# Turning every x chunk by DMA transpose, with the k weights on one queue, and moving the last LayerNorm tile and the w4 load

## The chip, the cores and the metric

The kernel runs on one core of a Trainium2 chip. The metric is the device time of one execution in microseconds (us), as measured for each run. The profiled execution also has a "span", the time from its first to its last recorded work; it is 1.5 to 2 us shorter than the measured time of the same run. All runs told of here were correct, and all are fast runs, that is, no run was over 1.5% above the fastest of the same kernel.

## The reference

The function mixes a linear attention branch A and a feed-forward branch B of the same input x by a sigmoid gate. S is 2048, D is 640, H is 32 heads of 20, F is 1728; everything is bf16.

```python
x = A_x                                       # [1, 2048, 640]
g = sigmoid((x * gate_w).sum(-1, keepdims=True))

# branch A
q, k, v = heads(x @ wqkv)                     # wqkv [640, 1920]
pq, pk = phi(q), phi(k)                       # phi(t) = where(t > 0, t + 1, exp(t)) + 1e-6
kv  = einsum("bhsd,bhse->bhde", pk, v)
z   = einsum("bhsd->bhd", pk)
num = einsum("bhqd,bhde->bhqe", pq, kv)
den = einsum("bhqd,bhd->bhq", pq, z)[..., None] + 1e-6
a   = merge_heads(num / den) @ wo

# branch B (its x is also A_x)
h  = gelu(layernorm(x) @ w1)
hs = shift_four_column_groups(h) @ w2         # rows shifted by +1, -1, +2, -2
x1 = x + hs
b  = x1 + gelu(layernorm(x1) @ w3) @ w4

return g * a + (1 - g) * b
```

## The kernel before

x is cut into 16 chunks of 128 rows, and into 4 tiles of 4 chunks. The k stage is `k = x @ wk`, and it needs x turned (`xT`, the 640 columns on the partitions) and wk in 5 pieces of 128 rows (`wk 0` to `wk 4`). It also produces the gate's logits, as a 641st column of wk that is filled from the gate vector `g5`. Below are the parts that matter; `sp`, `aq`, `gq` are the DMA queues of SP, ACT and POOL, and `pair()` gives one of 4 PSUM pairs (PSUM is the memory that matmuls write to). In the views PE runs the matmuls, DVE and ACT the elementwise work. LN1 is the LayerNorm of x and LN2 that of x1; their outputs `ln` are turned by DMA into `lnxT`. `den` is the denominator of the attention, `r_bf` its reciprocal, and an m unit computes one fifth of the product of `kv` and `wo`. The flight of a load is its time from issue to landing.

```python
    def load_x(c0, c1):        # plain load of chunks c0..c1, rows on partitions
        sp.dma_start(x_sb[:, c0:c1, 0:D], x2[c0 * P:c1 * P, :].rearrange("(c p) d -> p c d", p=P))
    def load_xT(c0, c1):       # DMA transpose of chunks c0..c1
        sp.dma_start_transpose(xT[:, :, c0 * P:c1 * P], x2[c0 * P:c1 * P, :])
    def load_wk(q, dc):        # one piece of wk, 160 KB
        q.dma_start(wk_sb[:, dc, 0:D], A_wqkv[dc * P:(dc + 1) * P, D:2 * D])

    load_x(0, 1)
    aq.dma_start(g5[:], gate_w.rearrange("(c p) -> c p", p=P))
    load_wk(sp, 1)
    load_wk(aq, 0)
    load_wk(aq, 2)
    load_wk(sp, 3)
    load_wk(aq, 4)
    for c0, c1 in ((1, 2), (2, 3), (3, 4), (4, 6), (6, 8), (8, 12), (12, 16)):
        load_xT(c0, c1)
    # ... wq, the rest of x, wv, w1, wo, w2, w3, all on sp

    def k_mm(pt, c, dcs, hfs=(0, 1), last=DC - 1):
        for dc in dcs:
            for hf in hfs:
                n = HD + hf
                nc.tensor.matmul(pt[:, hf, 0:n], lhsT=xT[:, dc, c * P:(c + 1) * P],
                                 rhs=wk_sb[:, dc, hf * HD:hf * HD + n], start=(dc == 0), stop=(dc == last))
    # ...
    warmup(6)                  # matmuls of ones, so that PE is busy while the loads fly
    warmup(3, P)
    kp = pair()
    # ... five PE transposes of x chunk 0 with two DVE copies into xT, and the gate vector turned by PE
    warmup(3, P)
    for dc in range(DC):
        k_mm(kp, 0, (dc,))
        if dc < DC - 1:
            warmup(1, 2 * P)
    k_evac(kp, 0)
    for c in range(1, NCH):
        pt = pair()
        k_mm(pt, c, range(DC))
        k_evac(pt, c)
    # ... the q stage, then the g stage (pk^T x), with LN1 of tiles 0 to 2 beside it

    def den_evac(pt):
        nc.scalar.activation(pt[:, 1, :], pt[:, 0, :], ACT.Copy, bias=1e-6)
        with nc.allow_low_precision(reason="rounded after a float32 division, as a copy would"):
            nc.vector.reciprocal(r_bf[:], pt[:, 1, :])

    def ln1_apply(c):          # "work" has 4 buffers
        # ...
        lnx = work.tile([P, D], BF16, name="ln")
        nc.vector.tensor_scalar(lnx[:], x_sb[:, c, 0:D], mv1[:, c, 0:1], rstd1[:, c:c + 1],
                                op0=ALU.subtract, op1=ALU.mult)
        nc.sync.dma_start_transpose(lnxT[t][:, :, cc * P:(cc + 1) * P], lnx[:])
    # ...
    for fcs in w1_split:
        w1_unit(0, fcs)
    kv_unit()
    den_evac(den_mm())
    for fcs in w1_split:
        w1_unit(1, fcs)
    for cc in range(CPT):
        ln1_apply(3 * CPT + cc)        # LN1 of the last tile
    s1.close()                 # frees the SBUF that w4_sb takes over
    # ... w4_sb allocated
    nc.gpsimd.dma_start(w4_sb[:, 0:FF, :], B_w4[0:FF * P, :].rearrange("(c p) f -> p c f", p=P))
    # ... two more loads for the rest of w4
    for j in range(DC):
        m_unit(j)              # each takes a PSUM pair; the second reuses den's
    r_unit()                   # reads r_bf
    # ... w2, w3, attention, w4 stages
```

## Time and profile before

| | before |
|---|---|
| time, median of 3 runs | 267.38 us (267.1 to 267.68) |
| span of the profiled run (266.56 us) | 264.9 us |
| PE busy | 260.5 us, 98% |
| first k matmul, chunk 0 done, chunk 1 done | 4.83, 7.19, 8.56 us |
| k stage ends, q stage begins on the chain | 27.80 us |
| reciprocal of den | 80.25 to 83.60 us |
| w2 stage begins | 88.28 us |

These lines are from the page of the kernel before: the busy time of the engines, the share by engine of the chain of waits (from the last instruction back, at each step to what released it), and the group of the k matmuls (busy us and mean ns of one, then the idle time just before them).

```profile
span 264.9 us, 4267 instructions
...
PE 260.5 (98%) x1744; PEld 162.6 (61%) x1744; DVE 139.6 (53%) x270; ACT 84.3 (32%) x122; POOL 22.7 (9%) x58
...
PE 97%; ACT 1%; DVE 0%; issue 0%
...
L190 PE MATMUL pp<-wk_sb,xT 128*128 128x320 bf16 (+1 forms) x160 | 23.0, 303 | 0.0
```

The kernel is a stream of matmuls. PE stood idle for 0.0 us before its 160 k matmuls. So no load was late for PE. What PE does at the start that is not useful are the warm-up matmuls.

The chain of waits of before, in order of time, shows the two places where the stream could be denser. Its columns are start us, us, and what.

```profile
0.83 3.04 PE pp L202 x9
...
5.03 0.54 PE pp L190 x2
...
7.09 20.71 PE pp L190 x152
27.80 21.58 PE pp L232 x100
...
85.03 0.69 PE pp L379 x16
85.74 2.49 ACT m_sb L381 x4
88.28 5.59 PE pp L415 x40
```

From 0.83 to 5 us (mostly cut here) there are only warm-ups and PE transposes. Then the five steps of chunk 0 run with a warm-up between each, and from 7.09 us on 152 k matmuls run without a break. At 85.7 us the chain is with ACT, which evacuates the m units.

The stretch from 3 to 5 us in the view by stretches shows what the DMA engines do while wk lands. The columns used here are the first (the stretch) and the last two: the mean busy share of the 16 DMA engines and what they moved in GB/s.

```profile
3.00:5.00 2.00, 2.00 (x15) 1.40 (x14) 0.71 (x3) 1.03 (x1) 1.67 (x6) 1.00 1.00 348
```

In this stretch the engines moved 348 GB/s.

The view of the tile wk_sb in before gives the flights of the five wk loads, shortest, median and longest:

```profile
DMA to landing us min/median/max: 3.1/3.8/4.0
```

The timeline of DVE around the reciprocal, before (start us, us, engine, line, operation, out<-in):

```profile
80.25 3.36 DVE L254 RECIPROCAL r_bf<-pp 128x512 bf16<-128x512 f32 x1
...
86.92 1.16 DVE L297 TENSOR_SCALAR ln<-x_sb,mv,rstd 128x640 bf16<-128x640 bf16 x3
88.28 0.45 DVE L297 TENSOR_SCALAR ln<-x_sb,mv,rstd 128x640 bf16<-128x640 bf16 x1 [0.20 <-DMA lnxT<-ln]
```

The reciprocal comes first and ends at 83.60. The four LN passes of the last tile come after it.

### The profile page before, as it was taken

Reading aid. Unit: us, or ns where it says so; the run is one execution under the profiler, and the core shown is the slowest. Engines: PE = TensorE matmul, PEld = TensorE weight load, DVE = VectorE, ACT = ScalarE, POOL = GpSimd, SP = SyncE. Lnnn points to the kernel's source line nnn. Section 1 sums busy time; section 2 is a strip of 40 time slices with the busy share of each in tenths; the row PEclk is TensorE's granted clock in tenths of the full one; section 3 lists DMA queues with packets and bytes.
Section 4 is the critical chain, followed back from the end, with each engine's and each line's share of the span. In section 5 each row is a group of like instructions: output and inputs, shape, how many; then the busy total and the mean of one; then the engine's idle time right before and its main releaser. Section 6 shows DMA issues by size and latency. Waiting matters only on the chain.

```text
span 264.9 us, 4267 instructions
## 1 busy us (share of the span) xinstructions
PE 260.5 (98%) x1744; PEld 162.6 (61%) x1744; DVE 139.6 (53%) x270; ACT 84.3 (32%) x122; POOL 22.7 (9%) x58
## 2 busy tenths in 40 slices
PE   8999999999999999999999999999999999999994
PEld 4777555788754644555666556567555566455663
DVE  1688778899856797955412364503464413122132
ACT  1555544321165635622420313330222340333100
POOL 7100010012223140001000001000001000000000
PEclk9999999999999999999999999999999999999999
DMA  7999989015668952000132000042000042000011
GB/s 194 148 182 350 369 293 330 9 33 121 125 97 217 228 105 52 0 0 2 25 74 77 25 0 2 11 88 77 25 0 2 1 99 74 27 0 2 0 50 50
DMA packets 44749, 23.62 MB, mean 89 GB/s; under 512 B 35450, under 2 KB 43642, under 8 KB 44730
## 3 DMA queue, kind: packets, MB, share of 16 engines
q1 hardware_dynamic: 43792, 20.57, 32.6%
q0 software_dynamic: 496, 2.29, 2.9%
q10 hardware_dynamic: 442, 0.49, 0.5%
q8 instruction: 13, 0.21, 0.3%
q14 instruction: 6, 0.05, 0.1%
HBM read 12.21 MB, written 2.62 MB: 56 GB/s over the span
## 4 chain that ended last, share of the span: by engine, by line
PE 97%; ACT 1%; DVE 0%; issue 0%
PE pp L479 22%; PE pp L462 21%; PE pp L190 8%; PE pp L307 8%; PE pp L415 8%; PE pp L446 8%; PE pp L341 8%; PE pp L232 8%; PE pp L202 2%; PE pp L467 1%; PE pp L488 1%; ACT m_sb L381 1%; PE pp L360 1%; PE pp L247 0%; PE pp L379 0%; PE pp L211 0%
## 5 line engine op out<-in xcount | busy, mean ns | idle before, releaser
L470 ACT ACTIVATE h<-pp 128x1024 bf16<-128x1024 f32 (+1 forms) x28 | 27.8, 993 | 102.8 <-PE pp L462 94.4
L462 PE MATMUL pp<-lnxT,w_sb 128*128 128x512 bf16 x260 | 60.4, 379 | 0.0
L479 PE MATMUL pp<-w_sb,h 128*128 128x320 bf16 x416 | 57.9, 299 | 0.0
L479 PEld LDWEIGHTS <-h 128*128 128x128 bf16 x416 | 40.0, 98 | 17.0 <-issue 1.9
L462 PEld LDWEIGHTS <-w_sb 128*128 128x128 bf16 x260 | 25.5, 98 | 26.7
L495 DVE SCALAR_TENSOR_TENSOR oc<-pp,omg,x 128x640 bf16<-128x640 f32 x15 | 12.9, 882 | 44.0 <-PE pp L488 27.1
L449 DVE SCALAR_TENSOR_TENSOR x<-pp,gate,x 128x640 f32<-128x640 f32 x16 | 13.9, 868 | 29.4 <-PE pp L446 29.4
L182 ACT ACTIVATE e<-pp 128x640 bf16<-128x640 f32 (+1 forms) x26 | 21.5, 827 | 9.6 <-PE pp L232 9.6
L446 PE MATMUL pp<-m_sb,pqT 128*128 128x320 bf16 x160 | 24.3, 299 | 0.0
L418 DVE TENSOR_TENSOR x<-pp,x_sb 128x640 f32<-128x640 f32 x16 | 13.1, 820 | 20.7 <-PE pp L415 20.7
L415 PE MATMUL pp<-w_sb,hsT 128*128 128x320 bf16 x160 | 23.9, 299 | 0.1
L190 PE MATMUL pp<-wk_sb,xT 128*128 128x320 bf16 (+1 forms) x160 | 23.0, 303 | 0.0
L307 PE MATMUL pp<-x_sb,pk 128*128 128x320 bf16 (+1 forms) x160 | 22.3, 300 | 0.0
L232 PE MATMUL pp<-xT,hsT 128*128 128x512 bf16 x100 | 21.7, 379 | 0.0
L307 PEld LDWEIGHTS <-pk 128*128 128x128 bf16 x160 | 18.8, 117 | 3.5
L415 PEld LDWEIGHTS <-hsT 128*128 128x128 bf16 x160 | 15.6, 98 | 8.2 <-issue 0.2
L446 PEld LDWEIGHTS <-pqT 128*128 128x128 bf16 x160 | 15.7, 98 | 7.7
L190 PEld LDWEIGHTS <-xT 128*128 128x128 bf16 x160 | 15.8, 99 | 6.1
L341 PE MATMUL pp<-lnxT,w_sb 128*128 128x512 bf16 x80 | 17.9, 379 | 0.0
L232 PEld LDWEIGHTS <-hsT 128*128 128x128 bf16 x100 | 11.8, 118 | 9.7
L277 POOL TENSOR_SCALAR rstd<-mv 128x4 f32<-128x4 f32 (+1 forms) x11 | 3.5, 318 | 147.5 <-DVE mv L283 147.5
L184 DVE SCALAR_TENSOR_TENSOR pk<-pp,e 128x640 bf16<-128x640 f32 x16 | 13.2, 825 | 1.7
(79 smaller groups left out, 192.9 us busy)
## 6 DMA issues: line engine op xcount, KB each, us to landing
out_dram<-oc SPq DMA_DIRECT2D x15, 160.0 KB, 1.8
w_sb<-in_B_w_dram SPq DMA_DIRECT2D x1, 2160.0 KB, 8.5
w_sb<-in_B_w_dram POOLq DMA_DIRECT2D x1, 2080.0 KB, 12.7
x_sb<-in_A_x_dram SPq DMA_DIRECT2D x2, 640.0 KB, 9.8
x_sb<-in_A_x_dram SPq DMA_DIRECT2D x1, 1120.0 KB, 8.5
wo_sb<-in_A_wo_dram SPq DMA_DIRECT2D x6, 160.0 KB, 9.2
hsT<-in_A_wqkv_dram SPq DMA_DIRECT2D x1, 800.0 KB, 6.0
m_sb<-in_A_wqkv_dram SPq DMA_DIRECT2D x1, 800.0 KB, 11.0
```

The costliest lines, as they stand in the source:

```text
L182: nc.scalar.activation(ev, src, ACT.Exp)
L184: nc.vector.scalar_tensor_tensor(dst, src, 0.0, ev, op0=ALU.max, op1=ALU.add)
L190: nc.tensor.matmul(pt[:, hf, 0:n], lhsT=xT[:, dc, c * P:(c + 1) * P], rhs=wk_sb[:, dc, hf * HD:hf * HD + n], start=(dc == 0), stop=(dc == ...
L232: nc.tensor.matmul(pt[:, t % 2, :], lhsT=wq_sb[:, dc, :].rearrange("p (m j) -> p j m", j=DC)[:, j], rhs=xT[:, dc, t * TS:(t + 1) * TS], st ...
L307: nc.tensor.matmul(pt[:, hf, 0:HD + hf], lhsT=w, rhs=x_sb[:, c, hf * HD:(hf + 1) * HD + hf], start=(c == 0), stop=(c == NCH - 1))
L341: nc.tensor.matmul(pt[:, i, :], lhsT=w, rhs=lnxT[t][:, dc, :], start=(dc == 0), stop=(dc == DC - 1))
L415: nc.tensor.matmul(pt[:, hf, 0:HD], lhsT=hsT[:, fc, 2 + c * P:2 + (c + 1) * P], rhs=w2_sb[:, fc, hf * HD:(hf + 1) * HD], start=(fc == 0), ...
L446: nc.tensor.matmul(pt[:, hf, 0:HD], lhsT=pqT[:, j, c * P:(c + 1) * P], rhs=m_sb[:, j, hf * HD:(hf + 1) * HD], start=(j == 0), stop=(j == D ...
L449: nc.vector.scalar_tensor_tensor(x1, pt[:, :, 0:HD], gate[:, c:c + 1], x1, op0=ALU.mult, op1=ALU.add)
L462: nc.tensor.matmul(pt[:, k, :], lhsT=w3_sb[:, dc, fc * P:(fc + 1) * P], rhs=lnT[:, dc, :], start=(dc == 0), stop=(dc == DC - 1))
L470: nc.scalar.activation(h2[:, 2 * i * TS:2 * i * TS + n], pt[:].rearrange("p h e -> p (h e)")[:, 0:n], ACT.Gelu_apprx_tanh)
L479: nc.tensor.matmul(dst, lhsT=st[t]["h2"][:, fc * TS + cc * P:fc * TS + (cc + 1) * P], rhs=w4_sb[:, fc, a:b], start=start and fc == 0, stop ...
```

## The change

The intent at the start is that x chunk 0 need not be turned by PE: a DMA transpose at the head of the SP queue brings it in turned. All of wk goes to the ACT queue, so that SP has only transposes, and PE does chunks 0 and 1 together, as the wk pieces land. In the middle, LN1 of the last tile moves ahead of the reciprocal. So that its transposes do not run beside the 2.2 MB load of w4, that load moves behind LN2 of tile 0, to the SP queue.

```diff
-    load_x(0, 1)
+    load_wk(aq, 0)
+    load_xT(0, 1)
     aq.dma_start(g5[:], gate_w.rearrange("(c p) -> c p", p=P))
-    load_wk(sp, 1)
-    load_wk(aq, 0)
-    load_wk(aq, 2)
-    load_wk(sp, 3)
-    load_wk(aq, 4)
+    for dc in range(1, DC):
+        load_wk(aq, dc)
     for c0, c1 in ((1, 2), (2, 3), (3, 4), (4, 6), (6, 8), (8, 12), (12, 16)):
         load_xT(c0, c1)
     sp.dma_start(wq_sb, wqkv_v[:, :, 0:D])
-    load_x(1, 8)
+    load_x(0, 8)
@@
     warmup(6)
-    warmup(3, P)
-    kp = pair()
-    # (cut: five PE transposes of x chunk 0 and two DVE copies)
+    warmup(2, P)
+    kp = [pair(), pair()]
     # (cut: the gate vector turned by PE, kept)
-    warmup(3, P)
-    for dc in range(DC):
-        k_mm(kp, 0, (dc,))
-        if dc < DC - 1:
-            warmup(1, 2 * P)
-    k_evac(kp, 0)
-    for c in range(1, NCH):
+    warmup(4, P)
+    for dc in range(3):
+        k_mm(kp[0], 0, (dc,))
+        warmup(1, 2 * P)
+    k_mm(kp[1], 1, (0, 1, 2))
+    for c in range(2):
+        k_mm(kp[c], c, (3,))
+    for c in range(2):
+        k_mm(kp[c], c, (4,))
+        k_evac(kp[c], c)
+    for c in range(2, NCH):
@@
     kv_unit()
+    for cc in range(CPT):
+        ln1_apply(3 * CPT + cc)
     den_evac(den_mm())
     for fcs in w1_split:
         w1_unit(1, fcs)
-    for cc in range(CPT):
-        ln1_apply(3 * CPT + cc)
     s1.close()
-    nc.gpsimd.dma_start(w4_sb[:, 0:FF, :], ...)      # and two more
@@  (in the w3 stage of tile 0, after ln2_apply)
+    nc.sync.dma_start(w4_sb[:, 0:FF, :], ...)        # and two more
```

More of the change, by code (lines that the diff above doesn't have):

```diff
@@ L204 @@
     warmup(6)
-    warmup(3, P)
-    kp = pair()
-    turns = [(pair()[:, 0, :].bitcast(BF16), a, b) for a, b in ((0, 2), (2, DC))]
+    warmup(2, P)
+    kp = [pair(), pair()]
     tg = warm[:, 0, :].bitcast(BF16)
-    for n, (ptb, a, b) in enumerate(turns):
-        for dc in range(a, b):
-            nc.tensor.transpose(ptb[:, (dc - a) * P:(dc - a + 1) * P], x_sb[:, 0, dc * P:(dc + 1) * P], ident[:])
-        nc.vector.tensor_copy(xT[:, a:b, 0:P], ptb[:, 0:(b - a) * P].rearrange("p (c s) -> p c s", c=b - a))
-        if n == 0:
-            nc.tensor.transpose(tg[:, 0:DC], g5[:], ident[0:DC, 0:DC])
-            nc.vector.tensor_copy(wk_sb[:, :, D], tg[:, 0:DC])
-    warmup(3, P)
-    for dc in range(DC):
-        k_mm(kp, 0, (dc,))
-        if dc < DC - 1:
-            warmup(1, 2 * P)
-    k_evac(kp, 0)
-    for c in range(1, NCH):
+    nc.tensor.transpose(tg[:, 0:DC], g5[:], ident[0:DC, 0:DC])
+    nc.vector.tensor_copy(wk_sb[:, :, D], tg[:, 0:DC])
+    warmup(4, P)
[9 more added lines that the diff above has]
+    for c in range(2, NCH):
         pt = pair()
@@ L395 @@
     w4_sb = w4p.tile([P, FF + 1, D], BF16)
-    nc.gpsimd.dma_start(w4_sb[:, 0:FF, :], B_w4[0:FF * P, :].rearrange("(c p) f -> p c f", p=P))
-    nc.gpsimd.dma_start(w4_sb[0:FR, FF, :], B_w4[FF * P:F, :])
-    nc.gpsimd.dma_start(w4_sb[FR:P, FF, :], B_w4[FF * P:F, :])
     h2p = ctx.enter_context(tc.tile_pool(name="h2p", bufs=1))
@@ L538 @@
             ln2_apply(0, CPT - 1)
+    nc.sync.dma_start(w4_sb[:, 0:FF, :], B_w4[0:FF * P, :].rearrange("(c p) f -> p c f", p=P))
+    nc.sync.dma_start(w4_sb[0:FR, FF, :], B_w4[FF * P:F, :])
+    nc.sync.dma_start(w4_sb[FR:P, FF, :], B_w4[FF * P:F, :])
     scale_t(0)
```

## The prediction

> **What bounds it now.** The page gives PE 98% busy of a 264.9 us span; the chain of waits is 97% PE: a matmul stream with two holes (timeline). (1) The start: warm-up matmuls from 0.83 us, first k matmul at 4.83, chunk 1 at 7.19. Ten k matmuls (one chunk) take 1.36 us, so 16 chunks are 21.8 us, but k ends at 27.80. (2) At 85.7-88.3 the chain hangs on ACT evacuating m (2.49 us). LN1, LN2 and the w4 load are nowhere on the chain.
>
> **What changes.**
>
> *Start.* The plain load of x chunk 0 (landed 2.30 us after issue), five PE transposes and two DVE copies go; chunk 0 becomes a DMA transpose at the head of the SP queue. SP loses three plain loads (0.4 us of issue each) and gains one transpose (1.3 us): later transposes are issued only 0.1-0.2 us earlier. The Trainium skill ("DMA: Bandwidth & Descriptors", Rules for kernel authors) says that spreading DMAs over queues adds no bandwidth and only saves issue time; here too wk landed 3.1-4.0 us after issue on either queue. In the built program wk 3 waits for wk 0 to land (estimate 3.2 us) and wk 4 for the gate vector, as completion semaphores are reused; so wk 4 lands at 6.0-7.3 (6.20 before). PE does chunks 0 and 1 together, both finished near 7.2 instead of 8.55: up to 1.3 us won.
>
> *Mostly lost again.* Transposes feed k with little spare: landings were 6.8, 7.3, 8.6, 10.75 (chunks 4, 5), 13.63 (6, 7), 16.54 (8-11), needed at 7.19, 8.55, 9.91, 11.28, 14.0, 16.73. Slack is 0.5 us at chunk 4, 0.4 at 6, 0.2 at 8. With landings 0.1-0.2 us earlier, about 0.4 us of the win survives chunk 8, unless the 1.5 us DMA stall seen at 11.8 does not recur.
>
> *LN1 tile 3 ahead of den.* Four DVE passes (1.5 us) now precede the 3.36 us reciprocal. They reuse buffers that the transposes of tile 2 read; the last of these lands at about 82 (estimate: issue 79.57 plus the usual 2.6; 88.18 before, beside the w4 load). Reciprocal ends at 85.0-86.0 rather than 83.6. Its PSUM pair is reused by the second m unit, which wants it at 85.6: cost 0-0.4 us. Gain on PE none: lnxT 3 landed at 95.2, needed at 99.1.
>
> *w4 behind LN2.* Issued near 102 on SP; 2.2 MB at the 360 GB/s seen for plain loads is 6.3 us (estimate), landing near 110, needed at 129.5. Nothing on PE.
>
> **Sum.** Start -0.4 (from -1.2 to +0.3), m stage +0.2 (0 to +0.5), on a median of 267.38, rounded down for the stall: **266.9 us, range 266.0 to 267.8**; faster over 2% 0.01, within 2% 0.98, slower over 2% 0.01.
>
> **What would show it.** Chunks 0 and 1 done near 7.2; then k matmuls waiting for xT at chunk 4, 6 or 8; k ending at 27.3-27.6. Reciprocal ending at 85-86, the second m unit right after it. w4 landing near 110. From the w3 stage on all equal, shifted.
>
> **What would make it wrong.** PE idles more between 4 and 7 us, so the full clock (granted at 5.99) may come later: "TensorE: Matmul & The Clock Gate", Part 1, asks for some 3.4 us of sustained activity; k matmuls at half clock take 0.27 instead of 0.136 us, so 2 us late costs 1 us. Chunk 0's transpose may land late among the wk loads. If the DMA stall moves, the whole 1.3 us could survive.

## The result

Before and after were run in turn, four times each. All ratios here are computed as the mean time of one kernel's runs over that of the other's of the same rounds, so they are not quite the ratio of the medians that are quoted.

| | before | after |
|---|---|---|
| time, median of 4 runs | 267.24 us (266.69 to 267.68) | 268.57 us (268.37 to 268.89) |
| ratio | | 1.0052, 95% interval 1.003 to 1.0074 |
| k stage ends | 27.80 us | 29.13 us |
| reciprocal of den ends | 83.60 us | 87.41 us |
| w2 stage begins | 88.28 us | 90.17 us |
| last matmul begins | 261.13 us | 263.02 us |

So the change is 0.5% slower. It lies within the 2%, but outside the predicted range, and the sign was wrong. The trace pair shows a larger gap (2.3 us of span) than the medians (1.3 us): the profiled run of before took 266.56 us, below its four runs here (in other rounds before went down to 266.2), and that of after 268.89 us, the slowest of its four. From the w2 stage to the last matmul the two traces differ by a constant 1.89 us. So everything happened before 90 us, and the remaining 0.4 us of span are in the tail behind the last matmul; that tail was not studied.

From the page of after:

```profile
span 267.2 us, 4246 instructions
...
PE 92%; DMA 4%; DVE 2%; issue 0%; ACTq 0%; DVEq 0%
...
L188 PE MATMUL pp<-wk_sb,xT 128*128 128x320 bf16 (+1 forms) x160 | 23.1, 304 | 1.2 <-DMA wk_sb<-in_A_wqkv_dram 1.2
```

The DMA now has 4% of the chain, and PE stands idle for 1.2 us before k matmuls, all of it for wk. The chain of waits of after:

```profile
1.20 2.35 DMA g<-in_gate_w_dram
...
3.56 5.75 DMA wk_sb<-in_A_wqkv_dram
...
9.35 19.78 PE pp L188 x144
29.13 21.58 PE pp L228 x100
...
80.93 2.66 DMA lnxT<-ln
...
83.69 0.45 DVE ln L293
84.14 3.28 DVE r_bf L250
...
87.46 2.36 PE pp L375 x64
...
90.17 5.59 PE pp L408 x40
```

There are two new waits. The first is wk 4: the ACT queue waits for the gate vector to land, issues wk 4 at 3.56, and the data takes 5.75 us to arrive, at 9.31. The two holes that this leaves in PE are in its timeline:

```profile
6.76 0.43 PE L188 MATMUL pp<-wk_sb,xT 128*128 128x320 bf16 x2 [0.53 <-DMA wk_sb<-in_A_wqkv_dram]
...
9.35 1.93 PE L188 MATMUL pp<-wk_sb,xT 128*128 128x320 bf16 x13 [0.69 <-DMA wk_sb<-in_A_wqkv_dram]
```

Chunks 0 and 1 were finished at 9.9 us, against 8.56 before. After that the k stage never waited again. In before, wk 4 was issued at 2.26 and landed at 6.20, so it took 3.94 us. The same stretch as above of the view by stretches, after:

```profile
3.00:5.00 2.00, 1.73 (x11) 1.09 (x10) 0.18 (x1) 0.80 (x1) 1.68 (x6) 1.00 0.89 163
```

The DMA engines are 89% busy and move 163 GB/s, less than half of the 348 of before. The packet records of the trace say more: the 1280-byte packets on the ACT queue (wk 0, 2 and 4 before, all of wk after) took 57.5 ns in the mean before and 94.6 ns after, in the first 10 us, and the first packet of a transpose ran at 2.27 us rather than 5.06.

The second new wait is in the chain at 80.93. The timeline of DVE, after:

```profile
81.44 1.34 DVE L293 TENSOR_SCALAR ln<-x_sb,mv,rstd 128x640 bf16<-128x640 bf16 x3
83.69 0.45 DVE L293 TENSOR_SCALAR ln<-x_sb,mv,rstd 128x640 bf16<-128x640 bf16 x1 [0.91 <-DMA lnxT<-ln]
84.05 3.35 DVE L250 RECIPROCAL r_bf<-pp 128x512 bf16<-128x512 f32 x1
```

The fourth LN pass waits 0.91 us for the last transpose of tile 2, whose buffer it reuses, and the reciprocal follows it. PE then waits for the reciprocal at the second m unit, as its timeline has it:

```profile
87.46 2.36 PE L375 MATMUL pp<-wo_sb,kvT 128*32 128x320 bf16 x64 [0.43 <-DVE r_bf L250]
```

In before all 80 matmuls of the five m units ran without a break:

```profile
84.97 2.90 PE L379 MATMUL pp<-wo_sb,kvT 128*32 128x320 bf16 x80
```

From the first matmul of q to the first of w2 PE took 60.64 us in before and 61.20 in after. So of the 1.89 us, 1.33 arose at the start and 0.56 in the middle.

The w4 load landed at 114 us and was first needed at 132 us.

### The profile page after: what moved, and what is told of

The parts are those of the page before. It is cut to its first block, busy times and chain, and to the rows that moved or that the text cites. A ratio compares the mean times of both kernels' runs of the same rounds, so it can differ in the third digit from the quotient of the medians.

```text
span 267.2 us, 4246 instructions
## 1 busy us (share of the span) xinstructions
PE 260.6 (98%) x1738; PEld 162.2 (61%) x1738; DVE 138.5 (52%) x268; ACT 84.2 (32%) x122; POOL 20.4 (8%) x55
## 4 chain that ended last, share of the span: by engine, by line
PE 92%; DMA 4%; DVE 2%; issue 0%; ACTq 0%; DVEq 0%
PE pp L472 21%; PE pp L455 21%; PE pp L303 8%; PE pp L408 8%; PE pp L439 8%; PE pp L228 8%; PE pp L188 7%; PE pp L337 6%; DMA wk_sb<-in_A_wqkv_dram 2%; DVE r_bf L250 1%; PE pp L460 1%; DMA lnxT<-ln 1%; PE pp L481 1%; PE pp L375 1%; DMA g<-in_gate_w_dram 1%; DVE hsT L347 0%
## 5 line engine op out<-in xcount | busy, mean ns | idle before, releaser
L228 PEld LDWEIGHTS <-hsT 128*128 128x128 bf16 x100 | 11.8, 118 | 9.7
L181 DVE TENSOR_SCALAR e<-e 128x640 bf16<-128x640 bf16 (+1 forms) x26 | 9.6, 368 | 11.2 <-ACT e L180 10.3
## 6 DMA issues: line engine op xcount, KB each, us to landing
w_sb<-in_B_w_dram SPq DMA_DIRECT2D x1, 2080.0 KB, 10.3
x_sb<-in_A_x_dram SPq DMA_DIRECT2D x2, 640.0 KB, 10.5
```

The lines of the kernel that those rows point to most:

```text
L228: nc.tensor.matmul(pt[:, t % 2, :], lhsT=wq_sb[:, dc, :].rearrange("p (m j) -> p j m", j=DC)[:, j], rhs=xT[:, dc, t * TS:(t + 1) * TS], st ...
```

## The experiments

Four theories were set up. The texts below use some of their letters.

- S: the loss at the start comes from the start part of the change alone, that is, from late wk; the middle part adds a second, smaller loss.
- B: the loss in the middle comes from the 4 LN buffers, which tie the reciprocal to a transpose.
- D: wk lands late because its loads now share the DMA engines with transposes that are in flight beside them, where before they were ahead of them.
- X, a rival of D: it is turning chunk 0 by DMA, rather than the loads of wk, that costs the time. Another rival of D is the later issue of wk 3 and wk 4 alone (they wait on completion semaphores which are used again).

Twelve kernels were run on four chips (no e8 is on record). The medians of before on them were 266.92 (e1 to e4), 266.86 (e5, e6, e7, e9), 266.63 (e10 to e12) and 266.83 (e13), of 11 runs each.

### The start alone, e1_start

The edit is the start of the change alone: the first two parts of the diff above, from the loads to the k loop. The middle stays as before.

> Only the start part of the change. Theory S (the start costs most of it): wk chunk 4 again lands near 9.3 us and the k stage again ends near 29.1 us in the trace (27.80 before), and the time is 0.8 to 1.4 us over before; from the q stage on everything is before, shifted, and the second m unit does not wait for the reciprocal. Rival M (the LN1 move is the main loss and the late start is one unlucky profile): within 0.4 us of before.

Measured: 267.7 us, ratio 1.0032 (1.0009 to 1.0055). The chain of e1_start shows the same wait, for wk 2:

```profile
2.35 4.50 DMA wk_sb<-in_A_wqkv_dram
...
8.82 19.78 PE pp L188 x144
28.60 21.58 PE pp L228 x100
```

PE waited 0.75 us for wk 1 and 0.68 us for wk 2, and the last 144 k matmuls start at 8.82. The reciprocal (81.05 to 84.41) made PE wait for nothing. From q to w2 it took 60.64 us, as before. The start part alone costs 0.32%, which is about 0.85 us, the lower end of what was expected, and q began on the chain at 28.60 us where 29.1 was expected. Theory S holds.

### The w4 move alone, e2_w4

```diff
-    nc.gpsimd.dma_start(w4_sb[:, 0:FF, :], ...)      # and two more, ahead of the m units
+    nc.sync.dma_start(w4_sb[:, 0:FF, :], ...)        # and two more, behind LN2 of tile 0
```

> Only the w4 load moved behind LN2 of tile 0. Both theories: no change on PE, within 0.3 us of before; the fourth LN1 transpose of tile 2 lands near 82 instead of 88.2 us, w4 lands near 112 and is needed at 129.5. If the w4 move itself costs anything (say, PE waiting for w4 or for LN2), the time is over 0.3 us longer.

Measured: 267.42 us, ratio 1.0007 (0.9986 to 1.0028). w4 landed at 112 us. It moves the time by nothing that can be seen. Its trace also warns of reading single traces: with the start of before unchanged, wk 4 took 4.57 us rather than 3.94 and the start was 0.44 us later.

### The LN1 move alone, e3_ln1

```diff
     kv_unit()
+    for cc in range(CPT):
+        ln1_apply(3 * CPT + cc)
     den_evac(den_mm())
     for fcs in w1_split:
         w1_unit(1, fcs)
-    for cc in range(CPT):
-        ln1_apply(3 * CPT + cc)
```

> Only the LN1 move, with the w4 load left early on POOL. Theory B (the reciprocal is held up because the fourth LN1 pass needs the buffer that the fourth transpose of tile 2 reads): that transpose lands near 88 us beside the w4 load, the reciprocal runs at 88.6 to 92.0, the second m unit starts then, and the time is 4 to 7 us over before. Rival (the move costs only the DVE time of four passes, 1.5 us, ahead of the reciprocal): reciprocal ends near 85.2, at most 0.3 us over before.

Measured: 275.14 us, ratio 1.0311 (1.0282 to 1.0341). This is slower by 8.2 us in the medians, somewhat more than expected; the clock explains the rest (below). In the chain of e3_ln1, both a line about the feed at the start and the middle are of use:

```profile
9.37 7.35 DMA xT<-in_A_x_dram
16.76 11.07 PE pp L190 x80
...
79.58 7.93 DMA lnxT<-ln
...
87.98 3.36 DVE r_bf L254
...
91.38 4.45 PE pp L379 x64
```

With w4 still loaded early from POOL, the last transpose of tile 2 flies beside it and takes 7.93 us, against 2.66 us in after. The fourth LN pass waits for its buffer, the reciprocal for the pass, and PE stands idle for 5.65 us. In this trace the granted clock then fell to half from 88.86 to 95.69 us, so that the 64 matmuls of the m units took 4.45 us rather than 2.36. PE worked 4.31 us at half clock, which costs about 2.15 us (an estimate); with the 5.65 us that makes the 7.8 us by which w2 began later than in before. All six runs have a mean clock of 0.987 or 0.988. So the w4 move, worth nothing by itself, is what makes the LN1 move bearable. It is also a first look at theory D in another place: a transpose beside a large plain load lands late.

The first two lines are a bonus. In this run the clock was granted early (3.53 us) and chunk 2 began at 8.09 (8.56 in before), yet q began at 27.67 (27.64 in before), because at chunk 8 the k matmuls waited for the transpose issued at 9.37. This is the "mostly lost again" of the prediction.

### LN1 and w4 moved, the start as before, e4_ln1_w4

The edit is e2_w4 and e3_ln1 together.

> The LN1 move and the w4 move together, with the start of before. Theory B: the fourth transpose of tile 2 lands near 82, the reciprocal ends near 86, the second m unit waits 0.4 us for it, and the time is 0.3 to 0.7 us over before. Rival: within 0.2 us. With e1_start the two excesses should add up to that of the whole change, 1.4 us.

Measured: 267.54 us, ratio 1.0022 (1.0002 to 1.0041). The reciprocal ran from 82.65 to 86.00, and PE waited 0.43 us for it. The losses of e1_start and e4_ln1_w4 are 0.32% and 0.22%, in sum 0.54%, and the whole change has 0.52%. So the two parts add up, as far as intervals of 0.2% to either side can tell. The trace took 61.20 us from q to w2, as after did.

### Two wk pieces on SP, between the transposes, e5_wk_split

Against e1_start:

```diff
     load_wk(aq, 0)
     load_xT(0, 1)
     aq.dma_start(g5[:], gate_w.rearrange("(c p) -> c p", p=P))
-    for dc in range(1, DC):
-        load_wk(aq, dc)
+    load_wk(sp, 1)
+    load_wk(aq, 2)
+    load_wk(sp, 3)
+    load_wk(aq, 4)
```

> The start of the change (chunk 0 by DMA transpose, chunks 0 and 1 together on PE), but wk 1 and 3 are issued on SP between the transposes of chunk 0 and chunk 1, as before put them ahead of its transposes; LN1 and w4 as before. Theory D (wk is late because the transposes of chunks 1 to 3 use the DMA engines at the same time): wk 4 lands at 6.0 to 7.0, the k stage ends 0 to 0.6 us after before's, time within 0.5 us of before. Rival X (turning chunk 0 by DMA is what costs): as e1_start, 0.8 us over before.

Measured: 268.28 us, ratio 1.0042 (1.0022 to 1.0061). The landing came out as expected of D: the last two pieces of wk landed at 6.34 and 6.86, and PE waited for wk only once, 0.41 us. The time did not follow. In the trace the transpose of chunk 1 was issued later (3.23) and landed at 7.46, and the full clock was granted only at 9.17; until then k matmuls started 0.267 us apart rather than 0.136. The runs fall into two groups, 267.35 twice and 268.19 to 268.6 four times. A late clock would make such groups, but when it was granted is on record for the profiled run alone, so this is not shown. (The mean clock of every run is on record too, 1.0 in the two fast ones and 0.997 to 0.999 in the others; in the profiled run that mean counts a fall of the clock at 265.17 us, near the end, and not the late grant.) The expectation on time was missed.

### The gate vector from another queue, e6_no_reuse_wait

Against e1_start:

```diff
-    aq.dma_start(g5[:], gate_w.rearrange("(c p) -> c p", p=P))
+    gq.dma_start(g5[:], gate_w.rearrange("(c p) -> c p", p=P))
```

> e1_start with the gate vector loaded from the POOL queue: wk 3 then waits for no semaphore and is issued at about 2.6 us instead of 3.1, wk 4 at about 3.1 instead of 3.6. Theory R (the late issue by semaphore reuse and one queue delays wk): wk 4 lands near 7.5 and the time is within 0.3 us of before. Theory D: wk 4 still lands after 8.5 us and the time is 0.5 to 0.9 us over before.

Measured: 268.94 us, ratio 1.0082 (1.0051 to 1.0113). The time says nothing, since the gate vector came late from POOL (5.03 us) and PE waited 1.38 us for it, and then 1.46 us more for the transpose of chunk 1, which took 6.34 us. The landing says something: wk 4 was issued at 3.23 rather than 3.56 and landed at 8.61, so it still took 5.38 us. Taking the gate vector off the queue brought the issue forward by 0.33 us only: wk 4 still waited for wk 0, which landed at 3.21, and in e10_hold, where it waited for no load, it was issued at 3.38. So most of the delay against before (2.26) comes from the loads ahead of it on the one queue.

### The start of before, with wk on ACT alone, e7_wk_act_only

```diff
+    load_wk(aq, 0)
     load_x(0, 1)
     aq.dma_start(g5[:], gate_w.rearrange("(c p) -> c p", p=P))
-    load_wk(sp, 1)
-    load_wk(aq, 0)
-    load_wk(aq, 2)
-    load_wk(sp, 3)
-    load_wk(aq, 4)
+    for dc in range(1, DC):
+        load_wk(aq, dc)
```

Chunk 0 is still loaded plain and turned by PE.

> Before with one part of the change alone: all wk on the ACT queue, so that the transposes of chunks 1 to 3 are issued on SP right behind the plain load of x chunk 0; chunk 0 is still turned by PE and done alone. Theory D: wk 4 lands at 8 to 9.3, chunk 0 ends about 2 us later than before, and the time is 1.3 to 2.3 us over before, more than e1_start, since nothing is done of chunk 1 meanwhile. Rival X (the transpose of chunk 0 is what costs): within 0.4 us of before.

Measured: 269.38 us, ratio 1.0097 (1.0075 to 1.0119). The chain of e7_wk_act_only:

```profile
1.21 3.40 DMA g<-in_gate_w_dram
4.63 4.88 DMA wk_sb<-in_A_wqkv_dram
9.55 20.87 PE pp L188 x152
```

Without any DMA transpose of chunk 0, wk is late all the same, and even more so. Rival X falls: the cost is in how wk is loaded. Landing and time are a little over what was expected of theory D, and the flight is not the main part here: wk 4 waited for the gate vector until 4.61 us, so that it was issued 2.4 us later than in before, and its flight was 0.9 us longer. The transposes on SP now start at 1.26 us, 0.9 us earlier than in before, since no wk load stands ahead of them.

### The opposite: chunks 0 and 1 by PE, e9_two_pe

```diff
     load_x(0, 1)
+    load_x(1, 2)
@@
-    for c0, c1 in ((1, 2), (2, 3), (3, 4), (4, 6), (6, 8), (8, 12), (12, 16)):
+    for c0, c1 in ((2, 3), (3, 4), (4, 6), (6, 8), (8, 12), (12, 16)):
@@  (further down, load_x(1, 8) becomes load_x(2, 8))
+    # (cut: five more PE transposes and a DVE copy for chunk 1)
-    warmup(3, P)
     for dc in range(DC):
-        k_mm(kp, 0, (dc,))
-        if dc < DC - 1:
-            warmup(1, 2 * P)
+        for c in range(2):
+            k_mm(kp[c], c, (dc,))
```

> The opposite of the change: chunks 0 and 1 both come by plain loads ahead of wk and are turned by PE, their k matmuls run together as wk lands, and one DMA transpose fewer is in the queue; the rest is before. If theory D and the reading of the feed are right: wk 4 lands at 6.3 to 7.0, both chunks end at 7.2 to 8.1 (8.55 before) depending on when the full clock is granted, the later transposes come 1 us earlier, and the time is 0.4 to 1.3 us under before. If the feed of transposes binds as the prediction said, the win is lost at chunk 4 to 8: within 0.3 us of before.

Measured: 267.71 us, ratio 1.003 (0.9999 to 1.0062), in two groups: 266.56, 266.74, 266.98 and 268.45, 268.69, 269.13. The profiled run is of the slow group. In it packets of the transposes that began at about 5.9 us took up to 2.1 us, from 6.4 to 7.8 us the DMA engines moved only 24 GB/s, and four of the five wk pieces landed at 7.25 to 8.33 (wk 4 took 6.07 us). This misses what was expected of theory D, although wk went ahead of the transposes. Why, and whether the fast group lacks this, is not known. A second loss of 1.23 us comes behind the start of w2 (see e13_merged_feed). The experiment is inconclusive, except that the kernel was not shown to be faster.

### Transposes held back until wk 1 has landed, e10_hold

Against e1_start:

```diff
+    hold = st1.tile([P, 16], BF16)
@@
     for dc in range(1, DC):
         load_wk(aq, dc)
+    sp.dma_start(hold[:], wk_sb[:, 1, 0:16])
     for c0, c1 in ((1, 2), (2, 3), (3, 4), (4, 6), (6, 8), (8, 12), (12, 16)):
         load_xT(c0, c1)
```

The small copy reads wk 1, so the SP queue waits for it before its next transpose. The ACT queue still issues all of wk. One thing changes besides: the semaphores are given out differently, so that wk 3 and wk 4 no longer wait for an earlier load.

> e1_start with the transposes of chunk 1 and later held back on SP until wk 1 has landed (a 4 KB copy on SP reads wk 1, so SP waits for it); wk stays on ACT alone, issued as in e1_start or 0.3 us sooner. It is not meant to be fast. Theory D: with no transposes beside it wk 4 lands 2.9 to 3.7 us after its issue, at 6.2 to 7.0, instead of 5.4 to 5.8 us after. Rival (one queue alone is what makes wk slow): wk 4 again takes over 5 us. In both, the transposes come some 3 us later and feed k too late: time 1.5 to 3.5 us over before.

Measured: 269.65 us (4 runs), ratio 1.013 (1.0082 to 1.0179). wk 4 was issued at 3.38, nearly as in after, and landed at 6.66: 3.28 us rather than 5.75. No piece of wk took more than 3.5 us (the 1.7 is the small copy):

```profile
DMA to landing us min/median/max: 1.7/3.3/3.5
```

This is the experiment that shows theory D: one queue, the same loads, nearly the same late issue, and of the transposes beside them only chunk 0's left. The stretch from 3 to 5 us of e10_hold has the DMA engines at 225 GB/s, though one transpose is still among the loads:

```profile
3.00:5.00 2.00, 1.65 (x12) 0.93 (x11) 0.18 (x1) 1.14 (x1) 1.68 (x6) 1.00 0.91 225
```

The time is worse because the transposes now come too late, as its chain shows:

```profile
1.99 3.42 DMA wk_sb<-in_A_wqkv_dram
5.42 0.54 SPq L132
...
9.96 4.20 DMA xT<-in_A_x_dram
...
14.21 16.55 PE pp L190 x120
```

PE waited 2.52 us for chunk 1 and then again for chunk 4. So the two needs pull against each other: transposes early enough for k slow wk down, and wk undisturbed makes the transposes late.

### Chunk 1 by PE, behind wk, e11_x1_pe

```diff
-    for c0, c1 in ((1, 2), (2, 3), (3, 4), (4, 6), (6, 8), (8, 12), (12, 16)):
+    load_x(1, 2)
+    for c0, c1 in ((2, 3), (3, 4), (4, 6), (6, 8), (8, 12), (12, 16)):
@@  (further down, load_x(1, 8) becomes load_x(2, 8))
+    tp = turns[0][0]
+    for dc in range(DC):
+        nc.tensor.transpose(tp[:, dc * P:(dc + 1) * P], x_sb[:, 1, dc * P:(dc + 1) * P], ident[:])
+    nc.vector.tensor_copy(xT[:, :, P:2 * P], tp[:, 0:D].rearrange("p (c s) -> p c s", c=DC))
+    warmup(4, 2 * P)
```

> A try for a faster kernel, from before: chunk 1 also comes by a plain load, issued on SP behind wk, and is turned by PE after the k matmuls of chunk 0; one DMA transpose fewer. wk 4 lands as in before, near 6.2; chunk 1 ends near 8.5 as in before, but the later transposes come 0.9 us sooner, so k should no longer wait for xT when the clock is granted early: 0 to 0.5 us under before.

Measured: 268.18 us, ratio 1.0055 (1.0025 to 1.0084). wk 4 took 4.27 us, no less than in before although the transposes were farther behind, and landed at 6.53. Once chunk 1 had begun, at 7.92, 150 k matmuls ran without a wait. But turning chunk 1 on PE, between chunks 0 and 1, cost more than it brought: q began at 28.37 (27.64 in before), and the kv stage waited 0.61 us for a transpose besides (from q to w2 it took 0.77 us more than before). The expectation on time was missed.

### The LN move with more buffers, e12_ln_bufs

Against e4_ln1_w4:

```diff
-    work = ctx.enter_context(tc.tile_pool(name="work", bufs=4))
+    work = ctx.enter_context(tc.tile_pool(name="work", bufs=8))
```

> e4_ln1_w4 with eight instead of four buffers for the LN1 output, so that no pass waits for a transpose of tile 2. Theory B (buffer wait, then the PSUM pair of den): the four passes end near 81.8, the reciprocal near 85.1, before the second m unit wants its pair, and the time is within 0.2 us of before. Rival (something else in the move costs): still 0.4 to 0.6 us over before, as e4_ln1_w4.

Measured: 267.07 us, ratio 1.0009 (0.9984 to 1.0034). The timeline of DVE in e12_ln_bufs:

```profile
80.28 1.51 DVE L297 TENSOR_SCALAR ln<-x_sb,mv,rstd 128x640 bf16<-128x640 bf16 x4
81.70 3.36 DVE L254 RECIPROCAL r_bf<-pp 128x512 bf16<-128x512 f32 x1
```

The four passes run without a break, the reciprocal ends at 85.06, and the second m unit follows the first without a wait, as the timeline of PE in e12_ln_bufs has it:

```profile
85.14 2.90 PE L379 MATMUL pp<-wo_sb,kvT 128*32 128x320 bf16 x80
```

From q to w2 it took 60.63 us, against 61.20 in e4_ln1_w4 and 60.64 in before. Theory B is shown by these traces: the loss in the middle was the buffers. (The intervals of the two times overlap and would not show it alone.) What remains of the LN move then is 0.09%, about 0.24 us where 0.2 was expected at most, with an interval around nothing.

### Fewer, larger transposes and no fill warm-ups, e13_merged_feed

```diff
-    for c0, c1 in ((1, 2), (2, 3), (3, 4), (4, 6), (6, 8), (8, 12), (12, 16)):
+    for c0, c1 in ((1, 2), (2, 4), (4, 6), (6, 8), (8, 12), (12, 16)):
@@
     for dc in range(DC):
         k_mm(kp, 0, (dc,))
-        if dc < DC - 1:
-            warmup(1, 2 * P)
```

> A try for a faster kernel, from before: the transposes of chunks 2 and 3 are one DMA, which saves about 1.1 us of issue on SP, so that all later chunks come that much sooner, and the four warm-up matmuls between the k matmuls of chunk 0 go (0.1 to 0.2 us each). If the feed of transposes is what keeps k from ending before 27.6 us (as in e3_ln1 and e4_ln1_w4, where the clock came early and k still ended there), k ends 0.2 to 0.6 us earlier: 0 to 0.5 us under before. If not, within 0.2 us.

Measured: 267.0 us, ratio 0.9992 (0.9959 to 1.0025). In its trace k ran from 6.90 without waits and q began 0.3 us earlier than in before, but the time is the same within the noise. The same trace loses 1.14 us behind the start of w2: with w4 loaded early, the last transpose of tile 2 took 12.1 us (8.6 in before), the fourth LN1 pass of tile 3 waited 3.87 us for its buffer, and PE then waited for DVE at 99.5 us. e9_two_pe has the same there (12.2 us). The w4 move takes away just this neighbour; a better start together with that move was not run, so it stays open whether the pair beats before. No kernel that was run does.

## Why the prediction was right or wrong

**The step that failed: "so wk 4 lands at 6.0-7.3 (6.20 before) ... up to 1.3 us won".** The late issue was foreseen (wk 4 waits for the gate vector, issued at 3.56). The duration was taken from before, "3.1-4.0 us after issue on either queue", which would have landed it at 6.7 to 7.6; it was 5.75, and wk 4 landed at 9.31. The reading of the Trainium skill behind it was right as far as it went: "DMA: Bandwidth & Descriptors", section "Issuing engines are not separate DMA queues", says that DMAs of all issuing engines run on the same 16 DMA engines and interleave. The prediction took from this that the queue does not matter. It follows just as well that a load interleaves with whatever else is in flight. In before, two wk loads stood on SP ahead of the transposes; the first transpose was issued at 2.19 us, but its packets ran only from 5.06 us, so wk had the engines nearly to itself. In after, a transpose stands first on SP, and packets of transposes run from 2.27 us on. A duration that was measured in one mix of traffic was used for another.

The flight of wk 4 (or of the last piece on ACT) sorts the runs:

| start | runs | flight of wk 4, us |
|---|---|---|
| wk ahead of the transposes | before, e2, e3, e4, e11, e12, e13 | 3.94, 4.57, 3.88, 4.08, 4.27, 3.94, 4.03 |
| wk ahead of all transposes but chunk 0's | e5 | 4.00 |
| wk on ACT, transposes beside it | after, e6, e7 | 5.75, 5.38, 4.88 |
| wk on ACT, transposes held back | e10 | 3.28 |

These are single traces: e7 (4.88) is hardly apart from e2 (4.57), and it is after, e6 and above all e10 that carry the argument. e9 is left out: with wk ahead of the transposes wk 4 took 6.07 us, for the stall told of above. So is e1, whose landing the semaphore records do not give; its last wk packet ended at 8.10 us and PE went on at 8.82, so the flight was 4.5 to 5.2 us. Of the landing that is 3.1 us later in after, 1.3 us are the later issue and 1.8 us the longer flight. The start then cost 0.32% (about +0.85 us, e1_start) where the prediction had -0.4 us. This is the mis-sized term, with its sign.

**"Chunks 0 and 1 both finished near 7.2": wrong** for the same reason; they were finished at 9.9 us.

**"Mostly lost again": right as a mechanism, but not put to work.** After the late wk, k never waited for xT again, since the feed had 1.3 us more to run ahead. Where the start was early (e3_ln1) or the transposes late (e10_hold), the feed did bind. That the gain which the change aimed for was small even with wk in time is argued from e3_ln1 and not shown.

**LN1 ahead of den: right in the mechanism, a little low in size.** The wait for the buffer of tile 2's last transpose, the reciprocal at the upper end of "85.0-86.0" (86.00 in e4_ln1_w4) and the wait of the second m unit are all there. The cost was predicted as 0 to 0.4 us with 0.2 in the sum, and measured as 0.22%, about 0.59 us by the ratio, with a wide interval; the traces have 0.43 us of wait on PE and 0.56 us more from q to w2. e12_ln_bufs removes it, and e3_ln1 shows that it is the w4 move which keeps it small.

**w4 behind LN2: right, with a wrong flight.** e2_w4 moves nothing; the load landed at 112 to 114 us, over 17 us before it was needed. Its flight was 10.1 to 10.3 us where 6.3 had been estimated; the slack was so large that this cost nothing.

**The clock: a true risk, but not the cause here.** It was granted at 6.15 us in after against 5.99, before both of PE's waits for wk. In the profiled run of e5_wk_split, at 9.17, it did hurt, and in e3_ln1 it fell to half after PE's long wait.

**The sum.** Predicted: -0.4 and +0.2, rounded down for the stall to 266.9 us. Measured: about +0.85 and +0.59, together the 1.4 us which the ratio of 1.0052 has. What stays open is the scatter of the start from run to run (the clock, and DMA stalls such as that of e9_two_pe), which is about as large as the effects that were looked for.

## What to carry to other kernels

In these runs the time from issue to landing of one and the same load (wk 4, 160 KB) went from 3.28 to 5.75 us with what flew beside it. When a change puts other traffic, above all DMA transposes, beside the loads that PE waits for, read a duration from a stretch with the same mix, or leave the order in the queue to protect them. Where a pass moves ahead of another on the same engine, look at the buffers it reuses: here four LN passes tied a reciprocal to a DMA transpose, and four more buffers freed it. And when a stage has two feeds (wk and xT here), a gain in the one is worth only what the other leaves.

## What the Trainium skill lacked or had wrong

- "Advanced Engine Details and Errata", section "X-Bar Transpose (TRN2)", says that transpose DMAs are as fast as regular ones, and expects 350 to 400 GB/s. Here transposes alone moved 276 GB/s (after, 9.5 to 10.5 us) and 289 GB/s (before, 13.4 to 14.4 us), plain loads alone 371 GB/s (before, 4 to 5 us), and both together 163 GB/s (after, 3 to 5 us). No stretch of 1 us in any trace, up to 22 us, had transposes alone at over 291 GB/s. The measurement decides.
- "DMA: Bandwidth & Descriptors", Rules for kernel authors, says that spreading loads over queues does not help and that a transpose next to ordinary DMAs needs nothing. The second is about correct data, and no run here contradicts it; but neither says that transposes make the plain loads beside them late (wk 4 took 3.94 us ahead of them, 5.75 beside them, 3.28 with them held back), or the reverse (2.66 us for a transpose, 7.93 to 12.2 beside a 2.2 MB load). In these runs the order in the queue was worth something for this reason.
- "TensorE: Matmul & The Clock Gate", Part 1, says that the warm-up varies from run to run, and the runs agree. Its advice that the ramp is too small to fit is of less use: with the same six warm-up matmuls from 0.83 us on, the full clock came between 3.49 us (e6_no_reuse_wait) and 9.17 us (e5_wk_split), and k matmuls started 0.267 us apart before and 0.136 us after it.
- No page tells of stretches in which DMA transposes stall and the engines move nearly nothing: in before packets that began at 11.8 us took up to 1.59 us, and 3 GB/s were moved from 12.2 to 13.2 us; in e9_two_pe packets that began at 5.9 us took up to 2.1 us, and 24 GB/s were moved from 6.4 to 7.8 us.
